# A rational activation on ScalarE and VectorE: the denominator as (|b1 h| + |b0|) * h with an absolute value behind it, in place of a square and a sum

## The chip, the core and the metric

One NeuronCore of a Trainium2 chip runs the whole program in one launch. The metric is device time in microseconds (us). The kernel before takes 1738.68 us, the median of three runs (1737.3 to 1738.88). Engines are named as in the profile: PE multiplies matrices, ACT is the scalar engine, DVE the vector engine, POOL the third elementwise engine (it reads and writes SBUF alone), SP issues the DMAs.

## The reference

Three blocks follow each other on 4608 tokens: an attention without softmax, a block with a rational activation (this case's "first block"), and a gated block.

```python
kv = einsum('bhsd,bhse->bhde', k, v);  o = einsum('bhsd,bhde->bhse', q, kv)
x = o / sqrt(mean(o*o, -1) + 1e-6) * g_norm          # 8 x 8 x 576 x 64 -> 4608 x 512
h = x @ w_in                                         # 4608 x 2048
P = a[0] + a[1]*h + a[2]*h**2 + a[3]*h**3
Q = 1.0 + abs(b[0])*abs(h) + abs(b[1])*h**2
x = (P / (Q + 1e-6)) @ w_out                         # 4608 x 512
out = (silu(x @ w_gate) * (x @ w_val)) @ w_out2
```

The change is in how |b0||h| + |b1|h² is made.

## The kernel before

The tokens are cut into 9 tiles of 512. The first stage, some 900 us of the program, is one loop of 144 steps (`for s in range(S1)`): step s is tile t = s // 16 and hidden block f = s % 16 of 128 columns. Each step issues on PE `h_mm(s)` (12 matmuls of 512 columns into the PSUM tile `ph`, each product in three parts from high and low halves of both operands), then `y_mm(s - 2)` (12 matmuls that add the activation of two steps ago into the output `y`), and some attention matmuls. Then `g_step(s)` works on the 128x512 tile `ph` of this step.

Each engine runs its own instructions strictly in the order in which the code issues them; semaphores that the tile framework sets hold an instruction until what it needs is done. There is no scheduler behind it. `ph` has two buffers, so have `e1`, `e2`, `e3` and `ghl`.

What a step does, with the names used below:

- ACT reads `ph` three times (lines 406 to 408): the **Square** into e1, the **Abs** |b0 h| into e2, the **Identity** (-a3 h - a2) into e3.
- `g_finish(s - 1)` finishes the step before on DVE with three operations, **F1** e1<-e1,e2, **F2** e3<-e3,na,e2 and **F3** e3<-e1,e3. Then `split` makes two halves of e3: the **hi copy** on ACT (ghl<-e) and the **lo subtraction** on POOL (ghl<-e,ghl), which PE needs for `y_mm(s - 1)`.
- The **sum** (line 414, on DVE) makes |b1| h² + |b0 h| in e1. ACT makes 1/sqrt(1 + sum) (the **rsqrt**, line 415) and squares it (the **second square**, line 416) into e2: that is 1/Q, which F1 and F2 of the next step need.
- DVE multiplies e3 by `ph` twice (lines 418 and 420).

Beside this runs the attention of the next tile, in a cycle of four steps (f % 4), one for each pair of heads. Step type 0: ACT squares `po` (sq) and copies it (sqhl), POOL subtracts sqhl. Type 2: ACT makes r and u from `ss`; DVE has u<-ss,u in front of the sum, r<-u,r behind it and u<-po,g_neg,r later; ACT copies the next q (qhl), and POOL subtracts it. Type 3: `x_attn` copies the finished x on ACT (x<-u, in front of the rsqrt) and subtracts its low half on POOL (x<-u,x). sq and u share one buffer, so the sq of the next type 0 waits for POOL's x. In step f = 13 of most tiles two more pairs of small copies and subtractions (kvh, kvl) come in.

The x of the last pair of heads is made in step f = 15, and `h_mm` of the next step, the first of the next tile, reads it in its last three matmuls. There are eight such tile boundaries.

In tile 0 DVE, ACT and POOL also convert two arriving weight blocks per step (wraw, wt). After the loop the gated block follows, which the change does not touch.

Of the kernel before, what the change touches and what calls it, by code (L numbers as in the profile page):

```python
# [12 lines left out]
AF = mybir.ActivationFunctionType  # L13
ALU = mybir.AluOpType
# [26 lines left out]
def fused_kernel(ctx: ExitStack, tc: tile.TileContext, kv_main, kv_left, q_t, w_in, w_out, w_gate, w_val, w_o2, ab, g_norm, out):  # L41
# [37 lines left out]
    ab_raw = const.tile([P, 6], F32, name="ab_raw")  # L79
    b_abs = const.tile([P, 2], F32, name="b_abs")  # L80
# [9 lines left out]
    def act(out, in_, func=AF.Copy, **kw):  # L90
        nc.scalar.activation(out=out, in_=in_, func=func, **kw)  # L91
# [8 lines left out]
    def stt(out, in0, scalar, in1, op0, op1):  # L100
        nc.vector.scalar_tensor_tensor(out=out, in0=in0, scalar=scalar, in1=in1, op0=op0, op1=op1)  # L101
# [25 lines left out]
    def join_ops(sts):  # L127
        views = [w_views(st) for st in sts]
        return [partial(stt, hi, hi, 3, lo, ALU.logical_shift_left, ALU.bitwise_or) for lo, hi, _ in views]
# [180 lines left out]
    def attn_head(c):  # L310

        T, i, ph = at(c)
        if ph == 0:
            st["sq"] = square(T, st["po"])
        elif ph == 2:
            norm_start(T, st["ss"])

    def attn_mid(c):
        T, i, ph = at(c)
        if ph == 0 and T >= 2:  # L320
            sub(nc.gpsimd, *st["sql"])
        elif ph == 3:
            x_attn(T, i, nc.gpsimd)
        return norm_ops(st["po"], st["ss"]) if ph == 2 else []
# [58 lines left out]
    def run(ops, k=1):  # L383
        for op in ops[:k]:
            op()
        del ops[:k]

    def g_finish(s, ops):
        if s not in mid:
            return  # L390
        e1, e2, e3 = mid.pop(s)
        stt(e1, e1, 1.0 + EPS_Q, e2, ALU.add, ALU.mult)
        stt(e3, e3, na[:, 0:1], e2, ALU.add, ALU.mult)
        run(ops)
        stt(e3, e1, 2.0, e3, ALU.subtract, ALU.mult)
        hl = g_p.tile([P, 2, N], F32R, tag="g", name="ghl")
        split(hl, e3, nc.gpsimd)
        hl_t[s] = hl

    def g_step(s, joins=()):  # L400
        ps = ew.pop(s)
        attn_head(s)
        e1 = e_p.tile([P, N], F32, tag="e1", name="e1")
        e2 = e_p.tile([P, N], F32, tag="e2", name="e2")
        e3 = e_p.tile([P, N], F32, tag="e3", name="e3")
        act(e1, ps, AF.Square)
        act(e2, ps, AF.Abs, scale=ab_raw[:, 4:5])
        act(e3, ps, AF.Identity, scale=na[:, 3:4], bias=na[:, 2:3])
        ops = join_ops(joins)
        g_finish(s - 1, ops)  # L410
        run(ops, len(ops))
        ops = attn_mid(s)
        run(ops)
        stt(e1, e1, b_abs[:, 1:2], e2, ALU.mult, ALU.add)
        act(e2, e1, AF.Abs_reciprocal_sqrt, bias=bias_q)
        act(e2, e2, AF.Square)
        run(ops)
        nc.vector.tensor_tensor(out=e3, in0=e3, in1=ps, op=ALU.mult)
        run(ops)
        stt(e3, e3, na[:, 1:2], ps, ALU.add, ALU.mult)  # L420
        mid[s] = (e1, e2, e3)
# [340 lines left out]
    with tc.manual_schedule():  # L762
# [90 lines left out]
        for s in range(S1):  # L853
# [16 lines left out]
            if t == 0 and f in (0, 3, 4, 7, 8, 11):  # L870
                pkv = ps_a.tile([P, HP, P], F32, tag="pa1", name="pkv")
                kv_b = (kv_jobs[kv_n[1]][0], pkv)
                for _ in range(HP):
                    kv_mm(pkv)
            g_step(s, raws[:2] if t == 0 else raw_u[0][f - 3:f - 2] if t == TILES - 1 and 3 <= f < 5 else ())
            if s >= LAG and f == LAG - 1:
                y_evac((s - LAG) // NF1, s_p, "stg")
# [244 lines left out]
```

## Time and profile before

| | |
|---|---|
| median of 3 runs | 1738.68 us |
| profiled execution, its own time | 1736.79 us |
| profiled execution, span from first to last instruction | 1735.0 us |
| PE busy | 1706.9 us (98%) |
| DVE busy | 1240.5 us (71%) |
| ACT busy | 1001.1 us (58%) |
| POOL busy | 508.0 us (29%) |

Busy shares over the span hide that the program has stages. In the first stage DVE is busy some 92% and PE 100% from 200 us on; in the gated block PE is busy 99% and DVE about half. A timeline row reads: start in us, duration in us, engine, line, operation, output<-inputs, and in square brackets the idle time in front of it with what ended that. A helper records many operations under its own line (L91 is `act`, L101 is `stt`, L94 is `sub`), so tiles' names tell them apart: e1, e2 and e3 all read as e there.

### The profile page before, as it was taken

The numbers are of one execution on the slowest core, as the hardware profiler recorded it, in microseconds if no ns is written. First come the engines' busy times: TensorE is split into PE (matmuls) and PEld (weight loads), VectorE is DVE, ScalarE is ACT, GpSimd is POOL, SyncE is SP. The second block draws the span as 40 slices with busy tenths as digits, with TensorE's granted clock in tenths as the row PEclk, the third lists the DMA queues.
The fourth block names the chain that finished last, engine by engine and source line by source line (L and its number), as shares of the span: only waits on it lengthen the run. The fifth ranks groups of instructions, "written<-read, shape, count | busy, mean of one in ns | idle before, by whom it ended". The sixth has DMA issues, their size and how long they took to land.

```text
span 1735.0 us, 21944 instructions
## 1 busy us (share of the span) xinstructions
PE 1706.9 (98%) x8112; PEld 1405.5 (81%) x8112; DVE 1240.5 (71%) x1625; ACT 1001.1 (58%) x1664; POOL 508.0 (29%) x363
## 2 busy tenths in 40 slices
PE   8988999999999999999999999999999999999999
PEld 5666888888888888888888888888888888888887
DVE  6999999999999998998886656666546766212211
ACT  6877787877878787777774434444424445112110
POOL 3555444444434343443332312222102212000000
PEclk9998999999999999999999999999999999999999
DMA  9762100010101000011107537122542255523411
GB/s 326 245 219 97 37 13 31 13 37 13 37 13 37 13 31 13 15 35 49 74 25 261 189 127 273 67 103 74 184 163 103 104 189 187 189 97 126 166 49 49
DMA packets 68682, 176.53 MB, mean 102 GB/s; under 512 B 7648, under 2 KB 10208, under 8 KB 66784
## 3 DMA queue, kind: packets, MB, share of 16 engines
q1 hardware_dynamic: 68576, 175.15, 28.7%
q8 instruction: 63, 1.03, 0.3%
q14 instruction: 43, 0.35, 0.1%
HBM read 117.44 MB, written 57.67 MB: 101 GB/s over the span
## 4 chain that ended last, share of the span: by engine, by line
PE 51%; issue 1%; DVE 0%; DMA 0%; POOL 0%; ACT 0%; SPq 0%; DVEq 0%; POOLq 0%; ACTq 0%
PE pb L105 10%; PE pb L106 10%; PE pb L107 10%; PE pb L752 6%; PE pb L750 6%; PE pb L751 6%; PE y L107 1%; PE y L106 1%; PE y L105 1%; PE ph L106 1%; PE ph L107 1%; PE ph L105 1%; DVE e L425 0%; DMA yraw<-yd 0%; POOL xc L94 0%
## 5 line engine op out<-in xcount | busy, mean ns | idle before, releaser
L94 POOL TENSOR_TENSOR ghl<-e,ghl 128x512 fp32r<-128x512 f32 x144 | 191.5, 1330 | 456.7 <-issue 193.6
L105 PE MATMUL pb<-xc,wu 128*128 128x512 f32 (+1 forms) x816 | 308.8, 378 | 1.1 <-DVE e L425 1.1
L106 PE MATMUL pb<-xc,wu 128*128 128x512 f32 (+1 forms) x816 | 308.6, 378 | 0.0
L107 PE MATMUL pb<-xc,wu 128*128 128x512 f32 (+1 forms) x816 | 308.6, 378 | 0.0
L101 DVE SCALAR_TENSOR_TENSOR e<-e,e 128x512 f32<-128x512 f32 x288 | 254.2, 883 | 30.8 <-ACT e L91 24.7
L106 PE MATMUL y<-ghl,wt 128*128 128x512 f32 x576 | 226.4, 393 | 5.5 <-POOL ghl L94 5.3
L105 PE MATMUL y<-ghl,wt 128*128 128x512 f32 x576 | 225.9, 392 | 5.3 <-ACT ghl L91 5.3
L105 PE MATMUL ph<-x,wt 128*128 128x512 f32 x576 | 228.7, 397 | 0.0
L106 PE MATMUL ph<-x,wt 128*128 128x512 f32 x576 | 226.2, 393 | 1.3 <-POOL x L94 1.3
L107 PE MATMUL y<-ghl,wt 128*128 128x512 f32 x576 | 226.0, 392 | 0.0
L107 PE MATMUL ph<-x,wt 128*128 128x512 f32 x576 | 225.3, 391 | 0.0
L425 DVE TENSOR_TENSOR e<-e,pb 128x512 f32<-128x512 f32 (+1 forms) x192 | 124.3, 652 | 139.4 <-PE pb L107 85.2
L91 ACT ACTIVATE e<-pb 128x512 f32<-128x512 f32 (+1 forms) x144 | 82.1, 570 | 233.0 <-PE pb L107 232.7
L105 PEld LDWEIGHTS pb<-xc,wu 128*128 128x128 f32 x816 | 153.3, 188 | 30.4 <-DVE e L425 1.7
L106 PEld LDWEIGHTS pb<-xc,wu 128*128 128x128 f32 x816 | 153.3, 188 | 28.6
L107 PEld LDWEIGHTS pb<-xc,wu 128*128 128x128 f32 x816 | 153.3, 188 | 28.6
L750 PE MATMUL pb<-wo,xc 128*128 128x512 f32 x432 | 168.0, 389 | 0.0
L751 PE MATMUL pb<-wo,xc 128*128 128x512 f32 x432 | 168.0, 389 | 0.0
L752 PE MATMUL pb<-wo,xc 128*128 128x512 f32 x432 | 168.0, 389 | 0.0
L91 ACT ACTIVATE e<-ph 128x512 f32<-128x512 f32 x144 | 85.5, 594 | 119.1 <-PE ph L107 118.7
L371 DVE COPY sb<-pb 128x512 f32<-128x512 f32 x18 | 12.4, 691 | 198.0 <-PE pb L752 198.0
L101 DVE SCALAR_TENSOR_TENSOR e<-e,na,e 128x512 f32<-128x512 f32 x144 | 149.4, 1037 | 0.0
(120 smaller groups left out, 3108.9 us busy)
## 6 DMA issues: line engine op xcount, KB each, us to landing
graw<-gd SPq DMA_DIRECT2D x108, 256.0 KB, 4.7
gd<-gout SPq DMA_DIRECT2D x84, 256.0 KB, 2.0
kvm<-in_kv_main SPq DMA_DIRECT2D x32, 512.0 KB, 8.9
yraw<-yd SPq DMA_DIRECT2D x26, 512.0 KB, 6.0
q<-in_q_t SPq DMA_DIRECT2D x36, 256.0 KB, 2.6
yd<-sb SPq DMA_DIRECT2D x18, 512.0 KB, 3.3
wraw<-in_w_in SPq DMA_DIRECT2D x16, 512.0 KB, 5.7
wraw<-in_w_out SPq DMA_DIRECT2D x16, 512.0 KB, 4.2
```

The source lines that it names most:

```text
L91: nc.scalar.activation(out=out, in_=in_, func=func, **kw)
L94: eng.tensor_tensor(out=out, in0=a, in1=b.bitcast(F32), op=ALU.subtract)
L101: nc.vector.scalar_tensor_tensor(out=out, in0=in0, scalar=scalar, in1=in1, op0=op0, op1=op1)
L105: nc.tensor.matmul(ps, lhsT=wh, rhs=xh, start=first, stop=False, skip_group_check=more)
L106: nc.tensor.matmul(ps, lhsT=wh, rhs=xl, start=False, stop=False, skip_group_check=more)
L107: nc.tensor.matmul(ps, lhsT=wl, rhs=xh, start=False, stop=last, skip_group_check=more)
L371: nc.vector.tensor_copy(out=sb[:, 1, :], in_=yps[2 * j + 1])
L425: eng.tensor_tensor(out=out, in0=a, in1=b, op=op)
L750: nc.tensor.matmul(b[m], lhsT=gh, rhs=w[:, 0, :], start=f == 0, stop=False)
L751: nc.tensor.matmul(b[m], lhsT=gh, rhs=w[:, 1, :], start=False, stop=False)
L752: nc.tensor.matmul(b[m], lhsT=gl, rhs=w[:, 0, :], start=False, stop=f == NF2 - 1)
```

## The change

ACT no longer squares `ph`. The Abs takes |b1 h| in place of |b0 h|. The sum becomes a product: (|b1 h| + |b0|) times `ph`, read by DVE from PSUM. That has the sign of h, so ACT takes its absolute value (**Abs'** below, e1<-e1) in front of the rsqrt.

```diff
-        act(e1, ps, AF.Square)
-        act(e2, ps, AF.Abs, scale=ab_raw[:, 4:5])
+        act(e2, ps, AF.Abs, scale=ab_raw[:, 5:6])
         act(e3, ps, AF.Identity, scale=na[:, 3:4], bias=na[:, 2:3])
         ops = join_ops(joins)
         g_finish(s - 1, ops)
         run(ops, len(ops))
         ops = attn_mid(s)
         run(ops)
-        stt(e1, e1, b_abs[:, 1:2], e2, ALU.mult, ALU.add)
+        stt(e1, e2, b_abs[:, 0:1], ps, ALU.add, ALU.mult)
+        act(e1, e1, AF.Abs)
         act(e2, e1, AF.Abs_reciprocal_sqrt, bias=bias_q)
         act(e2, e2, AF.Square)
```

PE's order is the same, and so is the number of instructions on every engine. On ACT, one step of type 0 of the first stage before (the first row is the Square; in brackets the engine whose semaphore the instruction waits for):

```order
L91 ACTIVATE e_4207<-ph 128x512 [waits PE_49]
L91 ACTIVATE e_4208<-ph,ab_raw 128x512
L91 ACTIVATE e_4209<-ph,na 128x512
L91 ACTIVATE ghl<-e_4161 128x512 [waits DVE_49]
L91 ACTIVATE e_4208<-e_4207,bias_q 128x512 [waits DVE_49]
L91 ACTIVATE e_4208<-e_4208 128x512 [waits Activation_49]
```

The same step on ACT in the changed kernel:

```order
L91 ACTIVATE e_4208<-ph,ab_raw 128x512 [waits PE_49]
L91 ACTIVATE e_4209<-ph,na 128x512
L91 ACTIVATE ghl<-e_4161 128x512 [waits DVE_49]
L91 ACTIVATE e_4207<-e_4207 128x512 [waits DVE_49]
L91 ACTIVATE e_4208<-e_4207,bias_q 128x512 [waits Activation_49]
L91 ACTIVATE e_4208<-e_4208 128x512 [waits Activation_49]
```

One instruction has moved from the front of the step to behind the hi copy, and there it waits for DVE's sum; the rsqrt now waits for ACT itself.

On DVE, the six operations of one step before (the sum, the two products with `ph`, then F1, F2 and F3):

```order
L101 SCALAR_TENSOR_TENSOR e_4763<-e_4763,b_abs,e_4764 128x512 [waits Activation_49]
L418 TENSOR_TENSOR e_4765<-e_4765,ph 128x512 [waits Activation_49]
L101 SCALAR_TENSOR_TENSOR e_4765<-e_4765,na,ph 128x512 [waits DVE_49]
L101 SCALAR_TENSOR_TENSOR e_4763<-e_4763,e_4764 128x512 [waits Activation_49]
L101 SCALAR_TENSOR_TENSOR e_4765<-e_4765,na,e_4764 128x512 [waits DVE_49]
L101 SCALAR_TENSOR_TENSOR e_4765<-e_4763,e_4765 128x512 [waits DVE_49]
```

The same six in the changed kernel:

```order
L101 SCALAR_TENSOR_TENSOR e_4763<-e_4764,b_abs,ph 128x512 [waits Activation_49]
L418 TENSOR_TENSOR e_4765<-e_4765,ph 128x512 [waits Pool_49]
L101 SCALAR_TENSOR_TENSOR e_4765<-e_4765,na,ph 128x512 [waits DVE_49]
L101 SCALAR_TENSOR_TENSOR e_4763<-e_4763,e_4764 128x512 [waits Activation_49]
L101 SCALAR_TENSOR_TENSOR e_4765<-e_4765,na,e_4764 128x512 [waits DVE_49]
L101 SCALAR_TENSOR_TENSOR e_4765<-e_4763,e_4765 128x512 [waits DVE_49]
```

The order is the same, and the sum now reads `ph`. Before, the product of line 418 waited for ACT (it needs the Identity's e3). [...]

## Rows read from the trace of the kernel before

**Rows 1.** The page's first line.

```profile
span 1735.0 us, 21944 instructions
```

**Rows 2.** Busy time of the engines in two stretches (us, busy, instructions, granted clock).

```profile
400.00:500.00 100.00, 100.00 (x451) 83.05 (x451) 91.59 (x118) 79.02 (x134) 44.17 (x34) 1.00 0.07 22
900.00:1735.00 835.00, 830.18 (x3777) 691.32 (x3775) 424.72 (x563) 301.41 (x477) 116.25 (x69) 1.00 0.39 140
```

**Rows 3.** Timeline of PE at the boundaries into tiles 1, 5 and 8.

```profile
170.38 0.50 PE L106 MATMUL ph<-x,wt 128*128 128x512 f32 x1 [1.11 <-POOL x L94]
...
539.99 0.39 PE L106 MATMUL ph<-x,wt 128*128 128x512 f32 x1
...
816.93 0.50 PE L106 MATMUL ph<-x,wt 128*128 128x512 f32 x1 [0.15 <-POOL x L94]
```

**Rows 4.** Timeline of POOL, last cycle of tile 4.

```profile
515.30 1.29 POOL L94 TENSOR_TENSOR x<-u,x 128x512 fp32r<-128x512 f32 x1
...
531.37 1.32 POOL L94 TENSOR_TENSOR ghl<-e,ghl 128x512 fp32r<-128x512 f32 x1 [2.25 <-issue]
533.11 1.29 POOL L94 TENSOR_TENSOR qhl<-q,qhl 128x512 fp32r<-128x512 f32 x1 [0.43 <-ACT qhl L91]
...
538.34 1.30 POOL L94 TENSOR_TENSOR x<-u,x 128x512 fp32r<-128x512 f32 x1
```

**Rows 5.** Groups by form, 150 to 780 us (busy us, mean ns; then idle).

```profile
L101 DVE SCALAR_TENSOR_TENSOR e<-e,b_abs,e 128x512 f32<-128x512 f32 x109 | 81.8, 751 | 22.5 <-ACT e L91 22.5
L101 DVE SCALAR_TENSOR_TENSOR e<-e,na,ph 128x512 f32<-128x512 f32 x108 | 80.5, 745 | 2.9
...
L91 ACT ACTIVATE e<-e 128x512 f32<-128x512 f32 x108 | 68.3, 633 | 3.4
L91 ACT ACTIVATE e<-ph 128x512 f32<-128x512 f32 x108 | 64.1, 594 | 88.2 <-PE ph L107 87.9
```

**Rows 6.** Timeline of DVE, last cycle of tile 4.

```profile
515.73 1.40 DVE L101 SCALAR_TENSOR_TENSOR e<-e,e 128x512 f32<-128x512 f32 x1 [0.46 <-ACT e L91]
517.06 0.74 DVE L101 SCALAR_TENSOR_TENSOR e<-e,na,e 128x512 f32<-128x512 f32 x1
517.83 0.69 DVE L101 SCALAR_TENSOR_TENSOR e<-e,e 128x512 f32<-128x512 f32 x1
...
521.44 0.69 DVE L101 SCALAR_TENSOR_TENSOR e<-e,e 128x512 f32<-128x512 f32 x1 [0.26 <-ACT e L91]
522.05 1.78 DVE L101 SCALAR_TENSOR_TENSOR e<-e,na,e 128x512 f32<-128x512 f32 x1
...
529.59 0.68 DVE L101 SCALAR_TENSOR_TENSOR u<-ss,u 128x512 f32<-128x512 f32 x1
530.19 0.74 DVE L101 SCALAR_TENSOR_TENSOR e<-e,b_abs,e 128x512 f32<-128x512 f32 x1
530.85 0.68 DVE L101 SCALAR_TENSOR_TENSOR r<-u,r 128x512 f32<-128x512 f32 x1
...
533.36 1.58 DVE L101 SCALAR_TENSOR_TENSOR e<-e,e 128x512 f32<-128x512 f32 x1
```

**Rows 7.** Timeline of ACT, step f = 14 of tile 4.

```profile
529.37 0.68 ACT L91 ACTIVATE e<-ph,ab_raw 128x512 f32<-128x512 f32 x1
529.93 0.78 ACT L91 ACTIVATE e<-ph,na 128x512 f32<-128x512 f32 x1
530.60 0.64 ACT L91 ACTIVATE ghl<-e 128x512 fp32r<-128x512 f32 x1
531.12 0.73 ACT L91 ACTIVATE e<-e,bias_q 128x512 f32<-128x512 f32 x1
531.88 0.63 ACT L91 ACTIVATE e<-e 128x512 f32<-128x512 f32 x1
532.41 0.62 ACT L91 ACTIVATE qhl<-q 128x512 fp32r<-128x512 f32 x1
```

**Rows 8.** Timeline of DVE in tile 0, the sum of step f = 6.

```profile
88.62 1.48 DVE L101 SCALAR_TENSOR_TENSOR e<-e,b_abs,e 128x512 f32<-128x512 f32 x1
```

## The prediction

> **What bounds the kernel now.** I read the busy shares by stage first. From 200 us on PE never stops: between 400 and 500 us it is busy 100.00 of 100 us at granted clock 1.00, with DVE at 91.59, ACT at 79.02 and POOL at 44.17; after 900 us it is busy 830.18 of 835 and DVE 424.72 [rows 2]. So no busy time that an engine gains here pays, and the change can only cost, unless it helps tile 0. What matters is whether PE starts to wait. PE's timeline shows where it nearly does: the last h matmuls of the first step of a tile need the x that POOL made in the step before. At the boundary into tile 1 PE waited 1.11 us for it, into tile 8 0.15 us [rows 3]; into tile 5 POOL's x ended at 538.34 + 1.30 = 539.64 and the matmul that needs it started at 539.99 [rows 3, 4], 0.35 us to spare. Inside a tile nothing is that close. The reader is to see eight such places, where lateness of x beyond some 0.3 us turns into PE time one for one.
>
> x is late when the step of type 3 is late, and that hangs on a loop of DVE and ACT: the sum (DVE), the rsqrt and the second square (ACT), F1, F2, F3 (DVE), the next sum. PE's own cycle of four steps is 538.34 - 515.30 = 23.04 us, read from POOL's x of two successive cycles [rows 4].
>
> **The loop before.** Sum 0.75 [rows 5]; rsqrt 0.73 and second square 0.63, each started 0.03 after what it needs (531.12 + 0.73 = 531.85, then 531.88) [rows 7]; F1 starts another 0.03 later and F2 0.61 after it (521.44, 522.05), F3 0.77 after F2 (517.06, 517.83) [rows 6], and the next sum again 0.61 on. That is 0.75 + 0.73 + 0.63 + 0.09 + 0.61 + 0.77 + 0.61 = 4.19 a step, 16.76 for four. Type 2 adds u<-ss,u, 0.60 (529.59 to 530.19) [rows 6]. POOL adds three holds: a DVE operation on two SBUF operands that starts while POOL runs ends 0.54 us after POOL does (533.36 + 1.58 = 534.94 behind POOL's 533.11 + 1.29 = 534.40) [rows 4, 6]. They are 1.40, 1.78 and 1.58 against 0.69, 0.74 and 0.69 [rows 6], together 2.64. The loop is 20.00 long, with 3.04 us a cycle to spare. A step that comes late is made good within a cycle.
>
> **The change part by part.** The Square from PSUM (594 ns) goes and an absolute value of e1 comes; the nearest row is the second square, an ACT operation on an SBUF tile with 633 ns [rows 5]. ACT has 0.04 us more a step, hidden in its 88.2 us of waiting for PE [rows 5]. The bounds of this unseen operation are those two rows; I take 0.63. The sum now reads PSUM; the nearest row is e<-e,na,ph with 745 ns, where the sum has 751 [rows 5]: no change in its own time, and I take 0.75. In none of its 108 instances was the mean of that form raised by POOL, so the new sum isn't held by POOL either.
>
> [...]
>
> What costs is the order. First, the sum waits for the Identity now, not for the Abs: in the changed order the product behind it has lost its wait for ACT. The Identity ends at 529.93 + 0.78 = 530.71, the Abs at 529.37 + 0.68 = 530.05 [rows 7], so 0.66 is lost there, and at most the Square's 0.59 [rows 5] is won in front: 0.07 later or a little more, counted from the end of h. Second, Abs' stands inside the loop: 0.63 + 0.03 = 0.66 a step, 2.64 a cycle, since the rsqrt needs its result. In type 3 the x copy stands between the hi copy and Abs' on ACT; at 0.52 each (530.60 to 531.12 [rows 7]) the two are done 0.03 + 1.04 = 1.07 after F3's end, where the sum is done 0.61 + 0.75 - 0.69 + 0.03 = 0.70 after it, so 0.37 more. Loop: 20.00 + 2.64 + 0.37 = 23.01 us, against PE's 23.04.
>
> [...]
>
> So the margin of 3.04 us a cycle falls to about nothing: PE can still keep its pace inside a tile, but a late step isn't made good before the tile ends.
>
> **How late x comes.** I walk steps 14 and 15 of tile 4. In step 13 ACT's chain ends some 0.5 later (Abs' waits for the sum), so kvh, r and u take the 0.5 that the missing Square leaves, and the Abs stays at 529.37, the Identity ends at 529.93 + 0.78 = 530.71, the hi copy stays at 530.60 and POOL's subtraction at 531.37 [rows 4, 7]. The sum starts at 530.74, not 530.19 [rows 6], and ends at 531.49; Abs' to 532.15, rsqrt to 532.91, second square 532.94 to 533.57. Before, that began at 531.88 [rows 7]: 1.06 later. The q copy behind it and POOL's q go from 533.11 to 534.17, until 535.46. On DVE r would start at 531.40, where before it started at 530.85, ahead of POOL's 531.37 [rows 4, 6]; now POOL is first, and r ends at 531.37 + 1.32 + 0.54 = 533.23. Three operations of 0.6 to 0.66 follow, F1 starts at about 535.1, meets POOL's q and ends at 535.46 + 0.54 = 536.00, against 534.94: 1.06 late, and hi copy and x follow by the same. If r slips in before POOL (0.03 us decide), F1 is free and F2 is held instead, until 535.77 + 0.54; F3 then ends about 0.7 late. So one cycle alone makes x 0.7 to 1.06 late. What the earlier cycles of the tile leave over comes on top, as the loop has no margin: between nothing and again that much. I take 1.05 for the one and 0.6 for the other, less 0.35 to spare: 1.3 us of waiting at a boundary, with ends of 0.35 (0.7 less 0.35) and 1.8.
>
> **Sum.** Eight boundaries by 1.3: 10.4 us. Tile 0 is paced by DVE; there four sums of type 2 were held by POOL like the one of 1.48 us [rows 8], and r would take most of that hold over, while the weight copies on ACT stand behind Abs' and come 0.56 later in 16 steps, in part behind DVE's own work. Ends: -4 x 0.73 = -2.9 and +16 x 0.56 = +9.0; I take +0.9, near the first, as DVE seldom waits for these copies. Together +11.3. The profiled execution took 1736.8 us itself (its span is 1735.0 [rows 1]), 1.9 below the median of the runs shown; so 1748.1 beside that one, and 1750.0 beside the median of 1738.7. Everything after the loop is bound by PE and starts later by the same.
>
> **Rivals.**
> - *PE never waits.* The margin does not vanish: with Square gone ACT's hi copy and POOL's subtractions come earlier, holds disappear (1.78 at 522.05 is one: POOL's sqhl could run before F1 gets there), and x keeps within its 0.35 us; or the sum isn't held by the Identity after all. For it: 3.04 us of margin were there. Against: the loop's 2.64 are counted, not guessed. 1738.7, or 1740 with one boundary late. Chance 0.11.
> - *Faster.* Tile 0 gives up its four holds (-2.9) and POOL's subtraction for y is no longer behind the sum's SBUF reads, which shortens PE's waits there; no boundary pays. Decides if x stays within its 0.35 us and DVE's pace in tile 0 gains more than the weight copies lose. 1734.5. Chance 0.04.
> - *The loop overtakes PE's cycle.* If the sum from PSUM or the waits between engines are some 0.1 us longer than the rows say, or one more hold comes in, the loop is 0.4 to 0.8 us longer than 23.04, PE waits in every cycle, 32 of them before the last tile: +13 to +26 on top of little else. 1764. Against: the nearest rows. Chance 0.12.
> - The forecast: x late at the boundaries. Chance 0.73.
>
> **How the numbers follow.** The forecast's own range is eight boundaries from 0.35 to 1.8 (2.8 to 14.4) with tile 0 between -1 and +4: 1740.5 to 1757. The range for eight in ten takes in the lower half of the third rival and leaves out the first two: 1741 to 1761. A measurement of this kernel can tell some 0.2% (3.5 us) from no change. Slower by more: the forecast and the third rival, 0.85. Within: 0.11. Faster: 0.04.
>
> **What would show it.** Right: PE waits of 1 to 2 us for POOL's x in the first step of the tiles, eight of them, where before there were two; F1's wait for ACT grows; between the boundaries PE is still full; Abs' is near 0.63 and the sum near 0.75; the sum starts behind the Identity's end. Wrong: no waits at the boundaries (first rival), PE waits for ghl in the middle of tiles (third), a sum clearly above 0.75, or the end of tile 0 moved by more than 3 us.

## The result, and the profile after

The changed kernel takes 1751.88 us in the median, the kernel before beside it 1738.78. The ratio is 1.0072, with a 95% interval of 1.0061 to 1.0084, so 12.5 us slower (10.6 to 14.6). One of the six executions ran at a mean granted clock of 0.847, where the others had 0.991 to 0.993, and took 1900.98 us; the ratio leaves it out, and the median of the other five is 1751.78. The profiled execution took 1753.44 us itself, 16.65 more than the one of before; it is 1.6 above its median, where that of before was 1.9 below its own.

The page's first lines, as in [rows 1], and the busy times (us, share, instructions):

```profile
span 1751.7 us, 21913 instructions
PE 1712.0 (98%) x8112; PEld 1406.6 (80%) x8112; DVE 1206.0 (69%) x1625; ACT 1030.8 (59%) x1664; POOL 491.6 (28%) x363
```

DVE and POOL became less busy (1240.5 to 1206.0, 508.0 to 491.6) while the kernel became slower: the two are held by each other for less time (in the mean F2 went from 1022 to 798 ns between 150 and 790 us and POOL's sqhl from 1764 to 1297 over the program, while r rose from 721 to 1705), and this pays nothing. Two stretches, as in [rows 2], the second from 918 us on, where that of before starts at 900:

```profile
400.00:500.00 100.00, 98.42 (x443) 81.28 (x442) 86.31 (x119) 81.94 (x134) 40.12 (x32) 1.00 0.07 22
918.00:1751.70 833.70, 828.81 (x3771) 690.18 (x3769) 424.82 (x563) 300.74 (x476) 116.60 (x69) 1.00 0.39 140
```

The gated block is as it was. In the first stage PE has lost 1.58 us of 100, and these are waits. What PE waited for, over the whole program (us in total, times, longest):

```profile
PE ph L106 <- POOL x L94: 10.1, 7, 1.6
PE y L105 <- ACT ghl L91: 8.7, 5, 2.5
PE y L106 <- POOL ghl L94: 4.8, 7, 0.9
```

The waits for ghl fall into tile 0, but for 0.2 us behind the last tile boundary; before they were 10.6 us together. The waits for x were 1.3 us before (the two in [rows 3]), so 8.8 us of the 10.1 are new. Three of the seven, at the boundaries into tiles 1, 5 and 8, as in [rows 3]:

```profile
174.53 0.51 PE L106 MATMUL ph<-x,wt 128*128 128x512 f32 x1 [1.57 <-POOL x L94]
...
552.77 0.50 PE L106 MATMUL ph<-x,wt 128*128 128x512 f32 x1 [1.38 <-POOL x L94]
...
832.93 0.50 PE L106 MATMUL ph<-x,wt 128*128 128x512 f32 x1 [1.54 <-POOL x L94]
```

Between them PE is full. The start of POOL's x at a tile's end, from tile to tile, shows how the time adds up. Before: 169.06 us, then after 92.39, 92.43, 92.03, 92.43, 92.58, 93.07 and 91.59 us more, and 919.42 to the end. After: 173.21, then 95.80, 94.12, 94.17, 94.14, 94.19, 93.00 and 92.98, and 920.09. So of 16.7 us in the span 4.2 come in tile 0, 11.9 in tiles 1 to 7, 0.7 later.

Tile 1 is 1.6 us longer than the four behind it, and that is PE's clock. Behind the waits at the end of tile 0 (2.50 and 0.85 us for ghl at 163.72 and 165.07 us, 1.57 for x at 174.53) the granted clock was 0.50 from 176 to 178 us, and eight matmuls started 0.42 to 0.43 us apart in place of 0.23. Behind the waits at 458.63 and 552.77 it stayed at 1.00. In the runs with one part of the change alone (tile 0, or tiles 1 to 8; below) tile 1 takes 92.40 and 94.14 us, without these 1.6.

The operations themselves, by form as in [rows 5] (busy us, mean ns; then idle):

```profile
L101 DVE SCALAR_TENSOR_TENSOR e<-e,b_abs,ph 128x512 f32<-128x512 f32 x108 | 80.2, 743 | 22.1 <-ACT e L91 22.1
L91 ACT ACTIVATE e<-e 128x512 f32<-128x512 f32 x214 | 135.0, 631 | 22.3 <-DVE e L101 17.8
L91 ACT ACTIVATE e<-ph,ab_raw 128x512 f32<-128x512 f32 x108 | 73.4, 679 | 14.2 <-PE ph L107 13.8
```

The sum from PSUM takes 743 ns (751 before), Abs' with the second square 631. ACT's waiting for PE in front of a step has gone from 88.2 us to 14.2: the loop of DVE and ACT now fills nearly all of PE's time.

How this looks in step 14 of tile 4, on ACT, as in [rows 7] (the Identity, the hi copy, Abs', the rsqrt, the second square):

```profile
541.93 0.77 ACT L91 ACTIVATE e<-ph,na 128x512 f32<-128x512 f32 x1
542.59 0.63 ACT L91 ACTIVATE ghl<-e 128x512 fp32r<-128x512 f32 x1
543.57 0.63 ACT L91 ACTIVATE e<-e 128x512 f32<-128x512 f32 x1 [0.35 <-DVE e L101]
544.24 0.72 ACT L91 ACTIVATE e<-e,bias_q 128x512 f32<-128x512 f32 x1
544.99 0.63 ACT L91 ACTIVATE e<-e 128x512 f32<-128x512 f32 x1
```

The rsqrt began 0.52 behind the hi copy in [rows 7]; now it begins 1.65 behind it. And on POOL, as in [rows 4]:

```profile
527.53 1.29 POOL L94 TENSOR_TENSOR x<-u,x 128x512 fp32r<-128x512 f32 x1
...
546.23 1.30 POOL L94 TENSOR_TENSOR qhl<-q,qhl 128x512 fp32r<-128x512 f32 x1 [1.57 <-ACT qhl L91]
...
551.44 1.27 POOL L94 TENSOR_TENSOR x<-u,x 128x512 fp32r<-128x512 f32 x1
```

From q to x it is 5.21 us, as before (538.34 - 533.11 = 5.23): the last step is late as a whole, and not stretched.

### The profile page after: what moved, and what is told of

The parts are those of the page before. It is cut to its first block, busy times and chain, and to the rows that moved or that the text cites. A ratio compares the mean times of both kernels' runs of the same rounds, so it can differ in the third digit from the quotient of the medians.

```text
span 1751.7 us, 21913 instructions
## 1 busy us (share of the span) xinstructions
PE 1712.0 (98%) x8112; PEld 1406.6 (80%) x8112; DVE 1206.0 (69%) x1625; ACT 1030.8 (59%) x1664; POOL 491.6 (28%) x363
## 4 chain that ended last, share of the span: by engine, by line
PE 47%; DVE 2%; ACT 2%; issue 1%; DMA 0%; POOL 0%; SPq 0%; DVEq 0%; POOLq 0%; ACTq 0%
PE pb L105 10%; PE pb L106 10%; PE pb L107 10%; PE pb L752 6%; PE pb L750 6%; PE pb L751 6%; DVE e L101 2%; ACT e L91 1%; PE y L106 0%; PE y L107 0%; PE y L105 0%; DVE e L425 0%; PE ph L106 0%; DMA yraw<-yd 0%; PE ph L107 0%
## 5 line engine op out<-in xcount | busy, mean ns | idle before, releaser
L94 POOL TENSOR_TENSOR ghl<-e,ghl 128x512 fp32r<-128x512 f32 x144 | 187.3, 1301 | 440.1 <-issue 216.7
L101 DVE SCALAR_TENSOR_TENSOR e<-e,e 128x512 f32<-128x512 f32 x288 | 225.5, 783 | 84.2 <-ACT e L91 79.6
L106 PE MATMUL ph<-x,wt 128*128 128x512 f32 x576 | 226.3, 393 | 10.1 <-POOL x L94 10.1
L91 ACT ACTIVATE e<-e 128x512 f32<-128x512 f32 x288 | 181.8, 631 | 34.9 <-DVE e L101 28.5
L107 PEld LDWEIGHTS pb<-xc,wu 128*128 128x128 f32 x816 | 153.3, 188 | 28.7
L91 ACT ACTIVATE ghl<-e 128x512 fp32r<-128x512 f32 x144 | 90.8, 630 | 103.2 <-DVE e L101 102.8
L371 DVE COPY sb<-pb 128x512 f32<-128x512 f32 x18 | 12.5, 692 | 198.1 <-PE pb L752 198.0
```

What stands on the lines that cost most here:

```text
L94: eng.tensor_tensor(out=out, in0=a, in1=b.bitcast(F32), op=ALU.subtract)
L106: nc.tensor.matmul(ps, lhsT=wh, rhs=xl, start=False, stop=False, skip_group_check=more)
L107: nc.tensor.matmul(ps, lhsT=wl, rhs=xh, start=False, stop=last, skip_group_check=more)
L371: nc.vector.tensor_copy(out=sb[:, 1, :], in_=yps[2 * j + 1])
```

## The experiments

All were timed in five rounds beside the kernel before, whose median was 1738.1 to 1739.5 us there. "Late" is against the kernel before.

**Abs' left out.** The changed kernel without its absolute value (so the root is of a signed number); the order, the PSUM read and the wait for the Identity stay.

```diff
-        act(e1, e1, AF.Abs)
```

> The changed kernel without the absolute value in front of the rsqrt (so 1/sqrt is taken of the signed product; the output is another). The sum still reads PSUM and still waits for the Identity. Theory (the absolute value inside the DVE-ACT loop costs its 0.66 us a step and makes x late at the tile boundaries): the loop has some 2.6 us a cycle to spare again, PE waits at most 0.2 us at a boundary, 1736 to 1740 us. Rival (the sum's wait for the Identity, or its reading PSUM, is what costs): the boundaries' waits of 1.2 to 1.6 us stay, 1747 to 1752 us.

1737.8 us, ratio 0.9997 (0.9986 to 1.0009). Without Abs' the price is gone whole. Two waits for x are left as before, but of 1.56 and 0.76 us and not of 0.2 at most. The forms of DVE, 150 to 790 us:

```profile
L101 DVE SCALAR_TENSOR_TENSOR e<-e,b_abs,ph 128x512 f32<-128x512 f32 x110 | 81.9, 745 | 31.1 <-ACT e L91 30.9
...
L101 DVE SCALAR_TENSOR_TENSOR r<-u,r 128x512 f32<-128x512 f32 x28 | 49.2, 1758 | 0.0
```

The sum waits for ACT and r is held by POOL just as in the changed kernel (1705 ns there, 0.68 us in [rows 6]), and neither costs anything while the loop has room.

**Abs' alone added** to the kernel before, behind the old sum, the Square kept.

```diff
+        act(e1, e1, AF.Abs)
```

> The kernel before, with the absolute value of the sum added between the sum and the rsqrt (it changes no number, as the sum is positive); the Square stays, and the sum reads SBUF and waits for the Abs alone. Theory: the loop is as long as in the changed kernel, x is late at the tile boundaries by 1 us or more, 1750 to 1758 us (ACT also has one operation more a step). Rival (the Identity's wait or the PSUM read costs): nothing but ACT's idle time is used, 1738 to 1741 us.

1755.5 us, ratio 1.0098 (1.0084 to 1.0112): Abs' by itself makes the whole loss and some more. The Square stays in front here, and the sum reads SBUF; no run says which of the two makes the rest. PE's waits for x are eight here:

```profile
PE ph L106 <- POOL x L94: 8.5, 8, 1.6
```

**r behind the two products,** in the changed kernel, so that POOL's lo subtraction no longer holds it.

```diff
-        run(ops)
         nc.vector.tensor_tensor(out=e3, in0=e3, in1=ps, op=ALU.mult)
-        run(ops)
         stt(e3, e3, na[:, 1:2], ps, ALU.add, ALU.mult)
+        run(ops, 2)
```

> The changed kernel with r<-u,r and u<-po,g_neg,r issued behind the two products with ph in steps of type 2, so that r starts when POOL's lo subtraction is over. Theory (r's hold of 1 us a cycle is one of the terms that make x late): r falls from 1705 to about 700 ns, the second square no longer has to be waited for less, F1 of type 2 comes 0.7 to 1 us earlier, boundary waits fall below 0.6 us each, 1741 to 1746 us. Rival (the hold lies in the shadow of ACT's chain, and the loop alone sets x): boundary waits stay at 1.2 to 1.6 us, 1750 to 1753 us.

1751.03 us, ratio 1.0071 (1.0058 to 1.0083): nothing gained, and PE still waits 8.2 us for x. DVE in step 14 and the start of step 15 of tile 4:

```profile
543.41 0.69 DVE L101 SCALAR_TENSOR_TENSOR r<-u,r 128x512 f32<-128x512 f32 x1
544.21 0.75 DVE L101 SCALAR_TENSOR_TENSOR u<-po,g_neg,r 128x512 f32<-128x512 f32 x1
544.88 1.77 DVE L101 SCALAR_TENSOR_TENSOR e<-e,e 128x512 f32<-128x512 f32 x1
```

r is free, and F1, which now starts earlier, waits out POOL's subtraction of q instead. The hold moves; the end of the chain doesn't.

**y before h** in the first step of tiles 1 to 8, so that the h matmuls ask for x 2.7 us later.

```diff
+            if t and f == 0:
+                y_mm(s - LAG)
...
-            if s >= LAG:
+            if s >= LAG and not (t and f == 0):
```

> The changed kernel with y_mm(s - 2) issued in front of h_mm(s) in the first step of tiles 1 to 8: PE has 2.7 us of other work before it needs x. Theory (inside a tile the loop keeps PE's pace, and only the lateness of x at the boundary is paid): the seven waits for x, 10.1 us together, go, 1740 to 1744 us. Rival (the loop is longer than PE's cycle, and the boundary is only where the deficit of a tile is paid): the same microseconds come back as waits for ghl or for x later on, 1748 to 1753 us.

1786.52 us, ratio 1.0275 (1.0261 to 1.0289). Neither theory. There is no wait for x any more, but PE now waits for ghl instead:

```profile
PE y L105 <- ACT ghl L91: 18.8, 12, 2.5
PE y L106 <- POOL ghl L94: 15.8, 23, 1.2
```

The new tile's first `ph` comes 12 matmuls later than it did, DVE's sums wait 50.5 us for ACT between 175 and 820 us (22.1 between 150 and 790 in the changed kernel), and a loop without room can't win it back: tiles 2 to 5 take 98.7 to 98.9 us, all of the excess in their first cycle (28.7 to 28.8 us from x to x, where the changed kernel has 24.1). How much of this is the wait for ghl and how much the idle loop was not taken apart.

**x earlier.** The x copy and POOL's x go to the head of the step of type 3, in front of F1 to F3; first in the changed kernel, then in the kernel before.

```diff
         elif ph == 2:
             norm_start(T, st["ss"])
+        elif ph == 3:
+            x_attn(T, i, nc.gpsimd)
...
-        elif ph == 3:
-            x_attn(T, i, nc.gpsimd)
```

> The changed kernel, with x made earlier: in a step of type 3 the x copy on ACT and its subtraction on POOL are issued at the head of the step (before the Abs of ph and before F1 to F3 of the step before) and no longer behind F3 and the hi copy. Theory (the price of the change is paid where the next tile's h matmuls wait for x, and nowhere else after tile 0): POOL's x ends before 550 instead of 552.71, the eight waits of PE for POOL's x at the tile boundaries fall from 10.1 us to under 2, and the time falls by 7 to 10 us to about 1743 (1740 to 1746), with only tile 0's share left. Rival (the loop of DVE and ACT has become longer than PE's 23.04 us a cycle, and x is only the place where it shows): x early lets PE go past the boundary, but then y's matmuls wait for ghl, or h comes late inside the tile, and the time stays at 1749 to 1754; POOL's x now runs beside F2 and may hold it by 0.6 us.

> The kernel before with the same move of x to the head of the step of type 3. Theory: of the two waits of PE for POOL's x (1.11 and 0.15 us) most goes, the loop has 3 us to spare, and x beside F2 costs nothing: 1736.5 to 1738.7, not to be told from before. Rival (POOL's x beside F1 to F3 is a new hold in the loop, and ghl comes late for y): 1741 or more.

In the changed kernel 1762.68 us, ratio 1.0136 (1.0122 to 1.0150); in the kernel before 1738.81, ratio 0.9994 (0.9985 to 1.0003). The first theory fell and its rival was too mild; the second held. In both, PE waits for x nowhere any more (in the changed kernel it waits for POOL's ghl instead, 14.2 us in 21 waits against 4.8 in 7), and in both POOL's x now runs beside F2 and holds it. In the changed kernel (DVE, then POOL):

```profile
555.79 1.04 DVE L101 SCALAR_TENSOR_TENSOR e<-e,e 128x512 f32<-128x512 f32 x1
556.75 1.79 DVE L101 SCALAR_TENSOR_TENSOR e<-e,na,e 128x512 f32<-128x512 f32 x1
```

```profile
485.25 1.74 POOL L94 TENSOR_TENSOR x<-u,x 128x512 fp32r<-128x512 f32 x1
508.61 1.74 POOL L94 TENSOR_TENSOR x<-u,x 128x512 fp32r<-128x512 f32 x1
531.95 1.76 POOL L94 TENSOR_TENSOR x<-u,x 128x512 fp32r<-128x512 f32 x1
556.22 1.77 POOL L94 TENSOR_TENSOR x<-u,x 128x512 fp32r<-128x512 f32 x1
```

and in the kernel before with x early (DVE):

```profile
533.18 1.66 DVE L101 SCALAR_TENSOR_TENSOR e<-e,e 128x512 f32<-128x512 f32 x1
534.76 1.78 DVE L101 SCALAR_TENSOR_TENSOR e<-e,na,e 128x512 f32<-128x512 f32 x1
```

The same 1.04 us more of F2 costs nothing with the old loop and 11 us with the new one. With x early in the changed kernel the loop itself is the bound, and its length can be read from x to x: 23.36 and 23.34 us in the two inner cycles of tile 4, against PE's 23.04, and 24.29 and 24.27 in the first and the last. So the ends of a tile are 0.93 longer than its middle. DVE shows why. In the first cycle it copies y out (sb<-y, two of 0.6), and in the last POOL's kvl holds F2 and F3 of step 13; the changed kernel in tile 4:

```profile
468.30 1.28 DVE L371 COPY sb<-y 128x512 f32<-128x512 f32 x2
...
539.91 1.22 DVE L101 SCALAR_TENSOR_TENSOR e<-e,na,e 128x512 f32<-128x512 f32 x1
541.17 1.12 DVE L101 SCALAR_TENSOR_TENSOR e<-e,e 128x512 f32<-128x512 f32 x1
```

against 0.74 and 0.69 unheld, together 0.91. A tile of four such cycles is 95.26 us, 2.8 longer than the 92.42 of the kernel before with x early. Seven such tiles, 1 to 7, would make 20; the two traces say 18.8 (663.7 against 644.9 us), as tiles 6 and 7 have shorter ends. The rest is tile 0, whose x starts 10.0 us later. The traces are 28.7 us apart as a whole; the medians are 23.9 apart.

**The new form in tile 0 alone, and in tiles 1 to 8 alone** (there the condition is s >= NF1; the Abs takes the scale that its form needs).

```diff
+        new = s < NF1
+        if not new:
+            act(e1, ps, AF.Square)
...
+        if new:
             stt(e1, e2, b_abs[:, 0:1], ps, ALU.add, ALU.mult)
             act(e1, e1, AF.Abs)
+        else:
+            stt(e1, e1, b_abs[:, 1:2], e2, ALU.mult, ALU.add)
```

> The new form (sum as a product with ph, Abs' behind it) in tile 0 alone, the 16 first steps; from tile 1 on the Square and the old sum. This prices the term of tile 0 by itself. Theory (by the traces of before and after, where the x of tile 0's end starts at 169.06 and 173.21): +4, so 1741 to 1744. Rival (the prediction's term, +0.9; the rest of the 4 us is scatter of the two profiled executions): 1738.5 to 1740.

> The counterpart: the old form in tile 0, the new one in the other eight tiles, so tiles 1 to 8. Theory (seven boundaries by 1.4 us, with the first boundary as in before): 1738.7 + 10 = 1748 to 1750, which with the run of tile 0 alone should add up to the 13 us of the whole change. Rival (tile 0 costs nothing of its own, and the whole change is the boundaries): 1751 to 1752.

Tile 0 alone: 1741.91 us, ratio 1.0016 (1.0008 to 1.0025), so 2.8 us (1.4 to 4.3), as the theory said and not the rival. Tiles 1 to 8 alone: 1750.07, ratio 1.0061 (1.0047 to 1.0074), so 10.6 us (8.2 to 12.9). Together 13.4, where the whole is 12.5 (10.6 to 14.6): the two add up. Tile 0's x starts at 173.39 and 168.12 in their traces.

**Half the number.** The kernel before with Abs' in the steps of types 0 and 1.

```diff
+        if s % 4 < 2:
+            act(e1, e1, AF.Abs)
```

> The kernel before (Square kept) with Abs' behind the sum in the steps of types 0 and 1 alone, half the number: the loop of DVE and ACT grows by 1.3 us a cycle to 21.3, still 1.7 under PE's 23.04, and types 2 and 3 in front of a tile's end are as before. Theory (the price comes from the used-up margin): no boundary waits, tiles of 92.4 us as in before, only tile 0 later by about half its 2.4 us: 1738.5 to 1741. Rival (each Abs' costs by itself, 13 to 17 us for 144): half of that, 1745 to 1748.

1745.06 us, ratio 1.0038 (1.0025 to 1.0050): the rival's number. Waits for x appear, six of 0.5 to 0.9 us behind the first one, which is as long as before (1.1):

```profile
PE ph L106 <- POOL x L94: 5.3, 7, 1.1
```

A margin of 3 us a cycle should have swallowed 1.3, so it was not there. The next two kernels and the table below look at the last steps of a tile.

**The new form in steps 12 and 13 alone, and in all but these.** The same code with another condition (the second kernel has `not in`):

```diff
+        new = s % NF1 in (12, 13)
```

> The new form in the steps f = 12 and 13 of every tile alone, 18 of 144 steps; the Square and the old sum in the others. Theory (from step 12 to the end of a tile DVE has almost no idle time left, so an Abs' there comes out at x, and one placed earlier is made good in its own cycle): with nothing carried in, F1 of step 13 comes some 0.9 us late, x by 0.8 to 0.9, which is 0.5 of waiting for POOL's x at each boundary; 8 x 0.5 and some 0.3 in tile 0 make 1742 to 1744.5. Rival (every Abs' costs the same wherever it stands, 13 us for 144): an eighth of it, 1740 to 1740.5.

> The counterpart: the new form in all steps but f = 12 and 13, so in 126 of 144. Theory: the chain comes into step 12 some 1.6 us late, as in the changed kernel, and makes 0.9 of it good in steps 12 and 13; x is 1.0 us late in place of 1.85, so the boundaries cost 0.6 to 0.7 each, and with 2.2 for tile 0 this makes 1744 to 1747. Rival (the same price for every step): seven eighths of 13, 1750.

The first: 1741.47 us, ratio 1.0019 (1.0010 to 1.0028), so 3.3 us (1.7 to 4.9), between the two numbers and no decision. Its trace speaks against the theory: PE's waits for x at the boundaries are 1.2 us in all, as before, and tiles 1 to 7 are 1.2 us longer together. Tile 0's x starts 5.7 us later there, and this single trace doesn't say how much of that is the edit. The second: 1749.41, ratio 1.0060 (1.0046 to 1.0074), the rival's number again. So it isn't the place of the two steps. What DVE does in step 13 of the first kernel shows how they are paid for (F1 of step 12 and what follows):

```profile
528.55 0.86 DVE L101 SCALAR_TENSOR_TENSOR e<-e,e 128x512 f32<-128x512 f32 x1 [0.74 <-ACT e L91]
529.33 0.74 DVE L101 SCALAR_TENSOR_TENSOR e<-e,na,e 128x512 f32<-128x512 f32 x1
```

In the second, where step 12 has the old form, as in the kernel before:

```profile
530.87 0.69 DVE L101 SCALAR_TENSOR_TENSOR e<-e,e 128x512 f32<-128x512 f32 x1 [0.25 <-ACT e L91]
531.48 1.78 DVE L101 SCALAR_TENSOR_TENSOR e<-e,na,e 128x512 f32<-128x512 f32 x1
```

F1 later by Abs' meets the end of POOL's sqhl in place of F2 meeting all of it: 0.49 us more of waiting for ACT, 0.87 less of hold.

Side by side, the last cycle of tile 4, in us from ACT's first read of `ph` of step 11 (a moment that PE sets in every one of them), and the tile's length from x to x:

| kernel | F1 of 11 | sum of 14 | x of 15 | x late | tile 4 |
|---|---|---|---|---|---|
| before | 4.53 | 18.99 | 27.14 | | 92.43 |
| new in 12, 13 | 4.53 | 19.51 | 27.51 | 0.37 | 92.68 |
| Abs' in types 0, 1 | 5.06 | 20.40 | 28.42 | 1.28 | 93.55 |
| new but in 12, 13 | 6.19 | 19.98 | 28.63 | 1.49 | 93.78 |
| after, r late | 6.09 | 20.26 | 28.91 | 1.77 | 94.02 |
| after | 6.20 | 20.36 | 28.99 | 1.85 | 94.14 |

The tile's length follows x's lateness within 0.2 us in all of them. The moment itself in the changed kernel:

```profile
522.45 0.69 ACT L91 ACTIVATE e<-ph,ab_raw 128x512 f32<-128x512 f32 x1 [0.27 <-PE ph L107]
```

ACT waits for PE at this point of every cycle of tile 4 but the last (0.23, 0.26 and 0.27 us): there the loop keeps up. It does no more than that. From one x of POOL to the next an inner cycle takes 23.07 and 23.08 us, and PE holds up none of the operations that follow one another on the way: the Abs of 522.45 and its Identity are done at 523.81, and DVE comes to their sum at 525.40. So this is the length of the loop itself.

**Tiles 6 and 7** have no kv operations (and tile 7 no q copy in its last cycle), and show what these cost. The last cycle of a tile, from x to x, is 23.90 to 23.93 us in tiles 1 to 5 of the changed kernel. In tiles 6 and 7 it is 22.76 and 22.74, and the 0.91 of hold by kvl is the larger part of the difference:

```profile
715.87 1.31 POOL L94 TENSOR_TENSOR x<-u,x 128x512 fp32r<-128x512 f32 x1
738.63 1.30 POOL L94 TENSOR_TENSOR x<-u,x 128x512 fp32r<-128x512 f32 x1
...
808.87 1.30 POOL L94 TENSOR_TENSOR x<-u,x 128x512 fp32r<-128x512 f32 x1
831.61 1.27 POOL L94 TENSOR_TENSOR x<-u,x 128x512 fp32r<-128x512 f32 x1
```

The boundary behind tile 6 is the one at which PE does not wait: PE itself takes 93.07 us for that tile (before) and the loop 93.00. For tile 7 PE takes 91.59 and the loop 92.98, and there PE waits 1.54 us.

The kernel before shows the same from the other side. In type 2 DVE's sum waits for ACT's Abs, which waits for PE, and this wait is the room of the cycle. Here it is in an inner cycle of tile 4, then in the last cycle of tile 6:

```profile
506.97 0.75 DVE L101 SCALAR_TENSOR_TENSOR e<-e,b_abs,e 128x512 f32<-128x512 f32 x1 [0.73 <-ACT e L91]
...
715.68 0.75 DVE L101 SCALAR_TENSOR_TENSOR e<-e,b_abs,e 128x512 f32<-128x512 f32 x1 [0.80 <-ACT e L91]
```

In the last cycle of tiles 1 to 5 the sum doesn't wait (530.19 in [rows 6]), and in no tile's first cycle, where DVE copies y out. So before the change a tile of the kind of tile 4 had some 0.7 us of room in each of its two inner cycles and none in the other two.

**Neither Square nor Abs'.** ACT takes the Abs scaled by the root of |b1|, and the sum is (that + |b0| over the root) times itself. The two factors, b_s, are made once.

```diff
-        act(e2, ps, AF.Abs, scale=ab_raw[:, 5:6])
+        act(e2, ps, AF.Abs, scale=b_s[:, 1:2])
...
-        stt(e1, e2, b_abs[:, 0:1], ps, ALU.add, ALU.mult)
-        act(e1, e1, AF.Abs)
+        stt(e1, e2, b_s[:, 0:1], e2, ALU.add, ALU.mult)
```

> A form without Square and without Abs': ACT takes the Abs of ph scaled by the root of |b1|, and DVE's sum is (that + |b0| over the root) times itself, which is |b1| h2 + |b0 h| with its sign right and needs no PSUM operand. ACT has one operation of 0.6 us less a step than either kernel, the loop is as long as before's 20.00, and the sum waits for the Abs alone. Theory: PE is the bound from tile 1 on, so at most tile 0 and the two small boundary waits can gain: 1735.5 to 1738.5, near before or a little under it. Rival (the earlier sum brings DVE's operations under POOL's subtractions, as the late r did): boundary waits appear, 1741 or more.

1738.78 us, ratio 0.9999 (0.9990 to 1.0008). One ACT operation fewer a step than either kernel, and no time won:

```profile
L93 ACT ACTIVATE e<-ph,b_s 128x512 f32<-128x512 f32 x108 | 74.4, 689 | 135.2 <-PE ph L109 134.1
```

What ACT saves, it waits for PE (88.2 us in [rows 5], 135.2 here). It beats the changed kernel by the whole loss and equals the kernel before; with PE full there is nothing for it to win.

## Why the prediction was right, and where it was not

Direction, size and place were right: 1750.0 was said, 1751.88 was measured, through PE's waits for x at the ends of tiles. The margin from which the size was worked out was wrong at both ends, and the errors cancelled; that part is luck. By its own steps:

- **PE is the bound, and x at a boundary is where lateness shows.** Right. Seven boundaries of eight wait, 1.19 to 1.58 us and 10.1 in all, where eight by 1.3, or 10.4, were summed. That sum left out that 1.3 us of such waits were there before; the waits grew by 8.8, and the slower clock in tile 1 adds 1.6. The run of tiles 1 to 8 alone puts 10.6 us (8.2 to 12.9) there.
- **Abs' in the loop is the cost; the rest of the change is free.** Right, and shown from both sides: without it 0.9997, with it alone 1.0098. Its 0.63 us and the sum's 0.75 came as taken from [rows 5].
- **The Identity's wait.** It is there (the sum at 542.81 starts 0.11 behind the Identity's end at 541.93 + 0.77; in all 144 steps of this trace it starts 0.03 us or more behind that end, where the old sum, which reads no `ph`, started 0.52 ahead of it, at 530.19 against 530.71 [rows 6, 7]) and free, as put outside the loop: the kernel without Abs' keeps it.
- **The loop 20.00 before and 23.01 after, PE 23.04.** The end is right for an inner cycle (23.07 and 23.08), the way to it is not. The loop before wasn't 20.00. Its inner cycle of 23.12 has 0.73 of waiting for PE, so the loop is 22.4 long (an estimate from these rows), and the margin 0.7 and not 3.04. The sum left out that DVE itself needs 533.36 - 530.19 = 3.17 us from the sum to F1 of type 2 [rows 6], where 2.20 were counted. It left out that in type 0 ACT's sq and sqhl stand in front of the Abs, and DVE's sum waits for it (0.45 us). And it took the x copy in front of the rsqrt for a new term of 0.37; it stands there in the kernel before too, and F1 at 515.73 has its 0.46 of waiting behind it [rows 6]. The kernel before in tile 4 (ACT's x copy and rsqrt of type 3, DVE's sum of type 0):

```profile
513.80 0.62 ACT L91 ACTIVATE x<-u 128x512 fp32r<-128x512 f32 x1
514.33 0.71 ACT L91 ACTIVATE e<-e,bias_q 128x512 f32<-128x512 f32 x1
...
518.98 0.75 DVE L101 SCALAR_TENSOR_TENSOR e<-e,b_abs,e 128x512 f32<-128x512 f32 x1 [0.45 <-ACT e L91]
```

  So the change adds not 3.01 but 0.7 to an inner cycle: Abs' of type 2 is hidden, since DVE's 3.17 are longer than ACT's chain of 2.86 with Abs', the 0.37 was paid already, and F2's hold by sqhl (1.78 at 522.05 in [rows 6]) goes, as the run of steps 12 and 13 shows.
- **One loop for all cycles.** Wrong. The first and the last cycle of tile 4 are 24.08 and 23.91 in the changed kernel, with the copies of y in the one and kvl in the other. So over a tile the loop is longer than PE: 94.1 to 94.2 us in tiles 2 to 5, where before they took 92.0 to 92.6. PE pays the difference once, at the boundary.
- **The walk of steps 14 and 15.** The sum was right, 1.65 late where 1.85 was measured; its parts were not. 1.05 was given to step 14 (r held by the lo subtraction, q later) and 0.6 to what comes in from earlier. The table says 1.37 comes in with the sum of step 14 and step 14 adds 0.5. Seen from `ph`, x is 0.98 late in an inner cycle too (527.53 - 522.45 = 5.08, before 515.30 - 511.20 = 4.10), where nobody waits for it; the last cycle adds 0.87. r is held as was said:

```profile
542.81 0.73 DVE L101 SCALAR_TENSOR_TENSOR e<-e,b_abs,ph 128x512 f32<-128x512 f32 x1
543.46 1.73 DVE L101 SCALAR_TENSOR_TENSOR r<-u,r 128x512 f32<-128x512 f32 x1
...
547.03 1.04 DVE L101 SCALAR_TENSOR_TENSOR e<-e,e 128x512 f32<-128x512 f32 x1
```

and for the reason given (POOL's lo subtraction ran from 543.35 to 544.65, and r was done 0.54 later). But F1's hold behind it fell from 1.58 [rows 6] to 1.04, and the r-late kernel shows that r's is no term of its own: a chain that comes 1.37 late waits for POOL either here or there. As r, F1, F2 and F3 have all been held by POOL in the rows shown (1.73 us for 0.68, 1.77 for 0.69, 1.79 for 0.74 and 1.12 for 0.69), what counts is when POOL is done. The walk's other branch (F2 held "until 535.77 + 0.54") rests on a time that none of its rows gives; with its own end of POOL's q, 535.46, F3 would come some 0.4 late and not 0.7, and the lower end of a wait would be near nothing.

- **Tile 0: +0.9.** Mis-sized: 2.8 (1.4 to 4.3), near the middle of its two ends and not near the first. DVE's waits for ACT between 20 and 170 us went from 5.9 to 8.9 us, half of that in front of the weights' operations and half in front of operations on e, and its waits for arriving weights from 4.1 to 5.8. No run separates them. In single traces tile 0's x starts between 165.9 and 169.1 us in the three kernels that have the old form there, and at 173.2 and 173.4 in the changed kernel and the run of tile 0 alone.
- **The rivals.** PE never waits: wrong for the changed kernel. Faster by tile 0: wrong, tile 0 lost. The loop overtakes PE: in part. Over a tile the loop is longer than PE's time, by some 1.7 us in tile 4, as that rival feared, but PE doesn't wait in every cycle: its only wait between 457.3 and 551.4 us is the one at the boundary. With one more hold in the loop, as the rival said, it costs 24 us (x early).

The same reading explains why half the Abs' operations cost half the price, and seven eighths nearly the whole. With Abs' in types 0 and 1 the four cycles of tile 4 are 23.88, 22.93, 22.94 and 23.80 us from x to x. The inner ones are still shorter than PE's 23.1 and win back 0.2 each; the first and the last, which had no room, are 0.7 to 0.8 longer than before. Together that is 93.55 in place of 92.43. Between F1 of step 13 and F3 of step 14 nothing can be won back, as DVE runs there without a gap in every kernel of the table. The kv operations were not moved in any run; what shows their part is five tiles with them against two without, in one trace. For the copies of y in the first cycle there is no such comparison.

## What to carry to other kernels

Count what an edit adds to the chain that goes round through two engines, not what it adds to either engine's busy time: here one engine got less work, the other 3% more, and 12.5 us were lost. Read the room of such a chain from its waits for the bound engine, cycle by cycle, and not as that engine's time less a sum of operations: the sum missed 2.4 of 22.4 us. Look for the cycle with the extra work (a copy out, a conversion) in front of the next point at which the bound engine must wait, and compare the edit with the room that is left in that one. And a stall between two engines that hold each other up is not a cost that can be removed by moving its victim: first see who comes next.

## What the runs showed of the hardware

- The sum takes DVE no longer with a PSUM operand: 743 and 745 ns with it (the changed kernel, and without Abs'), 751 and 753 from SBUF alone (the kernel before, and with neither Square nor Abs').
- The holds between DVE and POOL go both ways. POOL's x takes 1.29 us by itself [rows 4], and 1.74 to 1.77 where it starts while F1 is still running on two SBUF operands (x early in the changed kernel); F2 behind it is held in turn, 1.79 for 0.74. There the x started at 556.22 ends at 557.99, which is 1.16 after F1's end at 556.83, so all but 0.13 of its own time lies behind it.
- In the changed kernel's trace POOL reads and writes SBUF tiles alone in all of its 363 instructions.
- Moving 12 matmuls ahead of 12 others in eight of 144 steps, with the same work on every engine, cost 35 us beside the changed kernel, the largest loss of the study, without one wait for ghl on PE longer than 2.5 us.
